# A gated mix of two attention blocks on one core: whole token tiles at the start, fewer closing waits on SyncE, and denominators one group later

## The chip, the cores and the metric

The kernel runs on one core of a Trainium2 chip. A core has five engines that run their own instruction streams side by side: TensorE (PE; its weight loads are listed as PEld), VectorE (DVE), ScalarE (ACT), GpSimd (POOL) and SyncE (SP, which here issues most DMAs). They wait for one another on semaphores. The metric is the device time of one execution in microseconds, lower is better. All tensors are bfloat16; matmuls add up in float32 in PSUM.

## The reference

The input x (1 x 2048 x 1024) goes through two attention blocks of 32 heads of width 32, and the results are mixed by a gate per token:

```python
def _A_ref(x, wqkv, wo):                      # linear attention
    qkv = split_heads(x @ wqkv)
    phi = lambda t: jnp.where(t > 0, t + 1, jnp.exp(t)) + 1e-6
    pq, pk = phi(q), phi(k)
    kv = jnp.einsum("bhsd,bhse->bhde", pk, v)
    z = jnp.einsum("bhsd->bhd", pk)
    num = jnp.einsum("bhqd,bhde->bhqe", pq, kv)
    den = jnp.einsum("bhqd,bhd->bhq", pq, z)[..., None] + 1e-6
    return merge_heads(num / den) @ wo

def _B_ref(x, wqkv, wo):                      # sliding, dilated attention
    W, dil = 8, 2                             # keys at s, s-2, ..., s-14
    ...
    attn = _softmax(logits, axis=-1)
    o = jnp.einsum("bhsw,bhswd->bhsd", attn, vg)
    return merge_heads(o) @ wo

g = _sigmoid((x * gate_w).sum(-1, keepdims=True))
return g * _A_ref(x, A_wqkv, A_wo) + (1 - g) * _B_ref(x, B_wqkv, B_wo)
```

`split_heads` and `merge_heads` stand for the reshapes and transposes.

## The kernel before

**A recorded program with a planner.** `plan` records every operation with `P.op`: its engine, a cost, what it reads and writes, a priority and, for a DMA, a channel (`chan`) with a latency (`lat`). `Prog.schedule` then simulates the five engines with these costs and fixes the order on each one; a DMA is taken to land `lat` after the previous one and a constant 2.0 us more. `Prog.emit` writes the five streams with the semaphore waits that the order needs. Each DMA channel has its own semaphore. The planner runs six times and the shortest plan is kept. So costs and latencies are not code that runs; they only decide the order.

**Stages on PE.** All large products are groups of 8 matmuls of 128 x 512 (L1312), one PSUM bank each.

1. V of block B: 16 token tiles x 2 weight halves (256 matmuls). x comes transposed by DMA into `xT`, as 128-token tiles. Tiles 0 to 3 are loaded as two half tiles of 512 features each (L1299), in the order: first halves of tiles 0, 1, 2, 3, then second halves; tiles 4 to 15 are loaded whole by `load_x` (L1287). The first half of the weights (`load_w`, L1292) comes in four quarters of 256 KB that ACT issues at once; the second half comes in four more that ACT issues behind PE's groups on the first halves of tiles 0 to 3. The order of groups is tiles 0 to 7 on weight half 0, tiles 0 to 7 on half 1, then tiles 8 to 11 and 12 to 15 in the same way. Within tiles 0 to 3, PE does the first half tiles first. Nine matmuls on zeros (L1351) run before. Each group's bank is copied to an SBUF tile by ACT or DVE (L1344, L1343), which SP stores to HBM (L1378).
2. Q and K of block B, then K and V of block A, with the fills of the sliding attention between the groups (L1417, L1436, L1443) and block A's state (L1518).
3. The state is folded into the output weights (L1570). Then come the numerators of block A, 4 chunks of 512 tokens x 8 groups. `after(3, ...)` puts the denominators (L1597) of a chunk three groups behind its last numerator. `over(u)` then takes the reciprocals on ACT, writes them to HBM (L1605, 4 DMAs), reads them back spread over partitions (L1610, 8 DMAs into tiles `rb`), and DVE multiplies the chunk with them (L1613). Groups of `a_out` read the result.
4. The output groups (L1646), DVE's mix (L1650) and the stores of the output (L1656).

**The close.** A flag in SBUF tells whether the data fits the fast path. In `tail` each engine waits for the flag's operation, loads the flag (L1722) and branches (L1726): if the flag is 0, it runs a general path that stands behind the branch in its stream; else it jumps over it, to a drain and a barrier of all engines (L1732). SP, before its branch, waits for the semaphores of all DMA channels (L1725), two in one wait instruction:

```python
if eng == "sp":
    for s, v in P.final:
        e.wait_ge(s, v)
```

The general path starts with waits for all channels and all engines' counts; it does not run with this data.

Of the kernel before, what the change touches and what calls it, by code (L numbers as in the profile page):

```python
# [24 lines left out]
class Tile:  # L25
# [13 lines left out]
    def all(self):  # L39
        return [(self.space, self.lo, self.lo + self.row * self.size, self)]  # L40
# [15 lines left out]


class Op:
    __slots__ = ("eng", "fn", "cost", "deps", "prio", "seq", "chan", "lat", "pos", "val", "users", "raw", "name", "mode", "start", "end")


class Prog:
# [13 lines left out]
        self.held = {}  # L76
        self.read = set()

    def op(self, eng, fn, cost, reads=(), writes=(), prio=None, chan=None, lat=0.0, after=(), name="", mode="m"):
        o = Op()  # L80
        o.eng, o.fn, o.cost, o.prio, o.chan, o.lat, o.name, o.mode = eng, fn, cost, prio, chan, lat, name, mode
        if prio is None:
            o.prio = 1000 + len(self.ops)
        o.seq = len(self.ops)
        o.deps = set(after)
        o.raw = set(after)
        o.users = []
        rd = [iv for r in reads for iv in r]
        wr = [iv for w in writes for iv in w]
        for sp, lo, hi, own in rd:  # L90
            for rec in self.recs.get(sp, ()):
                if rec[0] < hi and lo < rec[1]:
                    if rec[3]:
# [24 lines left out]
        return o  # L118

    def schedule(self, dma_rate=0.2e6):  # L120
# [6 lines left out]
        dma_free = 0.0  # L127
# [20 lines left out]
        while done < len(self.ops):  # L148
            best = None
            for e in self.ENGS:  # L150
                while wait[e] and wait[e][0][0] <= free[e]:
                    _, _, o = heapq.heappop(wait[e])
                    heapq.heappush(avail[e], (o.prio, o.seq, o))
                if avail[e]:
                    t = free[e]
                elif wait[e]:
                    t = wait[e][0][0]
                else:
                    continue
                if best is None or t < best[0]:  # L160
                    best = (t, e)
            assert best is not None, "no operation can go"
            t, e = best
            if not avail[e]:
                while wait[e] and wait[e][0][0] <= t:
                    _, _, o = heapq.heappop(wait[e])
                    heapq.heappush(avail[e], (o.prio, o.seq, o))
            _, _, o = heapq.heappop(avail[e])
            if e == "pe":

                if o.mode != mode and mode != "m":
                    near = [x for x in avail[e] if x[2].mode == mode and x[0] < o.prio + 30]
                    if near:
                        x = min(near)
                        avail[e].remove(x)
                        heapq.heapify(avail[e])
                        heapq.heappush(avail[e], (o.prio, o.seq, o))
                        o = x[2]
                if o.mode != mode:
                    t += 0.09  # L180
                mode = o.mode
            o.start = t
            o.end = t + o.cost
            free[e] = o.end
            fin = o.end
            if o.chan is not None:
                dma_free = max(dma_free, o.end) + o.lat
                fin = dma_free + 2.0
            o.pos = len(self.order[e])
            self.order[e].append(o)  # L190
            done += 1
            for u in o.users:
                lat = self.LAT[o.eng] if (u.eng != o.eng or o in u.raw) and o.chan is None else 0.0
                if u.eng == o.eng == "pe":
                    lat = 0.0
                ready_at[u] = max(ready_at[u], fin + lat)
                left[u] -= 1
                if left[u] == 0:
                    ready(u, ready_at[u])
        self.span = max(free.values())  # L200

    def emit(self, block, tail):
        for e in self.ENGS:
# [40 lines left out]
            tail(e, eng)  # L244

        self.final = [(self.csem[c], n) for c, n in chan_n.items()]
        self.counts = cnt
        block.sync(lambda e: run(e, "sp"))
        block.scalar(lambda e: run(e, "act"))
# [853 lines left out]
def build_kernel(nc, A_x, A_wqkv, A_wo, B_x, B_wqkv, B_wo, gate_w, out):  # L1103
# [117 lines left out]
    def plan(seen):  # L1221
# [68 lines left out]
        def load_w(slot, half, src, c0, prio, d0=0, d1=8, eng="sp", after=()):  # L1290
            n = d1 - d0
            return P.op(eng, lambda e: e.dma_start(ws[slot][:, d0:d1, half * 512:half * 512 + 512], src[:, d0:d1, c0:c0 + 512]), 0.4 + 0.2 * n,  # L1292
                        writes=[ws[slot].part((d0, d1), (half * 512, half * 512 + 512))], prio=prio, chan="w%d_%d_%d" % (slot, half, d0), lat=0.55 * n, after=after)

        for d in range(0, 8, 2):
            load_w(0, 0, Bw, 2048, 0.1 + 0.1 * d, d, d + 2, "act")
        for b in range(2):
            for t in range(4):
                P.op("sp", lambda e, t=t, b=b: e.dma_start_transpose(xT[:, 4 * b:4 * b + 4, t * 128:(t + 1) * 128], x2[0, t * 128:(t + 1) * 128, 512 * b:512 * b + 512]),  # L1299
                     0.8, writes=[xT.part((4 * b, 4 * b + 4), (t * 128, (t + 1) * 128))], prio=4 * b + t, chan="x%d_%d" % (t, b), lat=0.6)  # L1300
        for t in range(4, NT):
            load_x(t, 8 + t)
        P.op("sp", lambda e: e.dma_start(gwb[:, :], gate_w[None, :].to_broadcast([128, D])), 0.6, writes=[gwb.all()], prio=29, chan="gw", lat=0.8)


# [44 lines left out]
        for i in range(WARM):  # L1350
# [2 lines left out]

        early = {(2, 0): (1, 0, Bw, 1024, 21), (4, 1): (2, 0, Bw, 0, 22), (7, 1): (1, 1, Bw, 1536, 23), (10, 1): (2, 1, Bw, 512, 24),
                 (12, 1): (3, 0, Aw, 1024, 25), (14, 1): (3, 1, Aw, 1536, 26)}
        for t, half in [(t, half) for t0, n in ((0, 8), (8, 4), (12, 4)) for half in range(2) for t in range(t0, t0 + n)]:
            vt, vs = vst.next()
            xs, xr = x_tile(t)
            w, wr = w_half(0, half)
            cuts = [0, 8]  # L1360
            if t < 4 and half == 0:
                cuts = [0, 2, 4, 6, 8] if t == 0 else [0, 4, 8]
                if t == 0:
                    first = [main.next() for _ in range(4)]
                    for t_ in range(4):
                        for d, d1 in ((0, 2), (2, 4)) if t_ == 0 else ((0, 4),):
                            group(first[t_], x_tile(t_)[0], w, [xT.part((d, d1), (t_ * 128, t_ * 128 + 128)), ws[0].part((d, d1), (0, 512))], d, d1)
                    o = P.ops[-1]
                    for d in range(0, 8, 2):
                        load_w(0, 1, Bw, 2560, 3 + 0.1 * d, d, d + 2, "act", after=[o])  # L1370
                cuts = cuts[len(cuts) // 2:]
                bank = first[t]
            else:
                bank = main.next()
            for d, d1 in zip(cuts, cuts[1:]):
                o = group(bank, xs, w, [xT.part((d, d1), (t * 128, t * 128 + 128)), ws[0].part((d, d1), (half * 512, half * 512 + 512))], d, d1)
            move(vt[:, :], bank.ap, 512, bank, vt.all())
            P.op("sp", lambda e, t=t, vt=vt, half=half: e.dma_start(vB_hbm[t * 128:(t + 1) * 128, half * 512:half * 512 + 512], vt[:, :]), 0.6, reads=[vt.all()],  # L1378
                 writes=[hb(t * 128, (t + 1) * 128, half)], chan="vst%d" % vs, lat=0.5, prio=5)
# [210 lines left out]
        def over(u):  # L1590
# [16 lines left out]
            for j in range(8):  # L1607
                B, bs = RBr.next()
                src = rc_hbm[u, 4 * j:4 * j + 4, :, :].rearrange("r k n -> (r k) n")[:, None, :].to_broadcast([16, 8, 512])
                last_in[0] = P.op("sp", lambda e, B=B, src=src: e.dma_start(B[:, :], src), 0.5, reads=[[("R", 4 * u + j // 2, 4 * u + j // 2 + 1, None)]], writes=[B.all()],  # L1610
                                  chan="rci%d" % bs, lat=1.0)
                dst, reg = tgt[:, j, c0:c0 + 512], tgt.part((j, j + 1), (c0, c0 + 512))
                P.op("dve", lambda e, B=B, dst=dst: e.tensor_tensor(dst, dst, B[:, :], ALU.mult), 0.65, reads=[reg, B.all()], writes=[reg])  # L1613

# [46 lines left out]
        for n, (u, j) in enumerate(nums):  # L1661
            numer(u, j)
            if j == 7:
                after(3, lambda u=u: over(u))
            slot(0)
            if n in (2, 4, 6, 8):
                fold((n - 2) // 4, (n - 2) // 2 % 2)
# [51 lines left out]
    def tail(e, eng):  # L1719
# [1 line left out]
        e.wait_ge(*flag_op.val)  # L1721
        e.reg_load(reg, flag[0:1, 0:1])  # L1722
        if eng == "sp":
            for s, v in P.final:
                e.wait_ge(s, v)  # L1725
        with e.If_eq(reg, 0):  # L1726
            for s, v in P.final + [(P.esem[x], n) for x, n in P.counts.items() if n]:
# [40 lines left out]
```

## Time and profile before

| | |
|---|---|
| three runs | 499.54, 501.1, 502.52 us (median 501.1) |
| the profiled execution's own time | 499.54 us |
| its span, first to last instruction | 497.7 us |
| PE busy | 484.9 us, 97% of the span |
| DVE, ACT, POOL busy | 274.1, 168.7, 5.1 us |
| granted TensorE clock | 1.000 |
| DMA, mean over the span | 98 GB/s |

The first row is what an execution takes without a profile. The profile lists one execution: its span lies inside the execution's own time, which is 1.84 us longer. Busy time is that of instructions that work; waits, branches and the issuing of DMAs are not counted in it. "Idle before" is the time in which an engine stood still just before an instruction, with what ended it behind an arrow. The first 40th of the span is 12.4 us long; in it PE is busy for 7 tenths, in the last for 5 tenths, and in all between for 9 tenths or more.

### The profile page before, as it was taken

The numbers are of one execution on the slowest core, as the hardware profiler recorded it, in microseconds if no ns is written. First come the engines' busy times: TensorE is split into PE (matmuls) and PEld (weight loads), VectorE is DVE, ScalarE is ACT, GpSimd is POOL, SyncE is SP. The second block draws the span as 40 slices with busy tenths as digits, with TensorE's granted clock in tenths as the row PEclk, the third lists the DMA queues.
The fourth block names the chain that finished last, engine by engine and source line by source line (L and its number), as shares of the span: only waits on it lengthen the run. The fifth ranks groups of instructions, "written<-read, shape, count | busy, mean of one in ns | idle before, by whom it ended". The sixth has DMA issues, their size and how long they took to land.

```text
span 497.7 us, 11467 instructions
## 1 busy us (share of the span) xinstructions
PE 484.9 (97%) x5121; PEld 226.2 (45%) x5121; DVE 274.1 (55%) x484; ACT 168.7 (34%) x290; POOL 5.1 (1%) x27
## 2 busy tenths in 40 slices
PE   7799999999999999999999999999999999999995
PEld 2344444444454444554554454444444444444442
DVE  2211425887777777556554645596865734524443
ACT  1011121133334445565655556355423322020000
POOL 3000000000000000000000000000000000000000
PEclk9999999999999999999999999999999999999999
DMA  8989994133003026301100100501664316101121
GB/s 169 215 192 286 359 353 117 43 107 105 1 24 107 24 79 186 79 24 39 31 24 23 36 12 4 168 3 31 162 190 100 92 24 166 58 8 66 63 86 68
DMA packets 51195, 48.80 MB, mean 98 GB/s; under 512 B 20289, under 2 KB 39105, under 8 KB 51138
## 3 DMA queue, kind: packets, MB, share of 16 engines
q1 hardware_dynamic: 48962, 45.89, 33.0%
q10 hardware_dynamic: 2176, 2.10, 1.9%
q8 instruction: 42, 0.69, 0.6%
q14 instruction: 15, 0.12, 0.1%
HBM read 34.34 MB, written 9.44 MB: 88 GB/s over the span
## 4 chain that ended last, share of the span: by engine, by line
PE 93%; SPq 2%; DMA 2%; DVE 1%; issue 0%
PE ps_all L1312 76%; PE ps_all L1646 11%; PE ps_all L1417 2%; SPq L1299 2%; PE ps_all L1436 2%; DMA xT<-in_A_x_dram 2%; PE ps_all L1518 1%; PE ps_all L1443 1%; DVE zsel L1560 1%; PE ps_all L1597 0%; DVE pq L1325 0%; SPq L1287 0%; PE ps_all L1570 0%; DVE e L1323 0%; DVE w L1343 0%
## 5 line engine op out<-in xcount | busy, mean ns | idle before, releaser
L1312 PE MATMUL ps_all<-w,xT 128*128 128x512 bf16 x960 | 213.9, 379 | 5.9 <-DMA xT<-in_A_x_dram 5.9
L1312 PE MATMUL ps_all<-xT,w 128*128 128x512 bf16 x768 | 170.7, 379 | 0.0
L1312 PEld LDWEIGHTS ps_all<-w,xT 128*128 128x128 bf16 x960 | 91.1, 98 | 115.0 <-DMA xT<-in_A_x_dram 8.5
L1312 PEld LDWEIGHTS ps_all<-xT,w 128*128 128x128 bf16 x768 | 73.7, 98 | 89.1 <-issue 1.8
L1646 PE MATMUL ps_all<-w,qT 128*128 128x512 bf16 (+1 forms) x264 | 55.6, 373 | 0.0
L1646 PEld LDWEIGHTS ps_all<-w,qT 128*128 128x128 bf16 x264 | 25.9, 98 | 29.6
L1323 DVE TENSOR_SCALAR e<-e 128x512 bf16<-128x512 bf16 x64 | 18.3, 290 | 34.6 <-ACT e L1321 17.3
L1343 DVE CAST vst<-ps_all 128x512 bf16<-128x512 f32 x16 | 11.1, 692 | 46.7 <-PE ps_all L1312 46.7
L1423 ACT ACTIVATE E<-ps_all 128x1824 bf16<-128x1824 f32 (+1 forms) x18 | 30.4, 1688 | 9.8 <-PE ps_all L1417 9.0
L1321 ACT ACTIVATE e<-ps_all 128x512 bf16<-128x512 f32 x32 | 19.1, 597 | 42.7 <-PE ps_all L1312 41.6
L1426 DVE TENSOR_TENSOR E<-E,msk 128x1824 bf16<-128x1824 bf16 (+1 forms) x18 | 19.8, 1102 | 22.1 <-ACT E L1423 22.1
L1650 DVE SCALAR_TENSOR_TENSOR o<-ps_all,gm,xT 128x512 bf16<-128x512 f32 (+1 forms) x25 | 18.2, 730 | 23.0 <-PE ps_all L1646 22.8
L1319 ACT ACTIVATE e<-ps_all 128x512 bf16<-128x512 f32 x32 | 19.1, 597 | 26.8 <-PE ps_all L1312 25.8
L1344 ACT ACTIVATE vst<-ps_all 128x512 bf16<-128x512 f32 x16 | 9.5, 597 | 51.1 <-PE ps_all L1312 51.1
L1455 DVE TENSOR_TENSOR qT<-ps_all,L 128x456 bf16<-128x456 f32 (+1 forms) x36 | 21.0, 626 | 6.2 <-ACT L L1453 5.0
L1274 DVE TENSOR_TENSOR mx<-mx,qT 128x1024 bf16<-128x1024 bf16 x32 | 20.9, 687 | 4.2 <-ACT qT L1347 4.0
L1274 DVE TENSOR_TENSOR mx<-mx,kT 128x1024 bf16<-128x1024 bf16 x32 | 20.9, 687 | 3.4 <-ACT kT L1344 3.2
L1344 ACT ACTIVATE kT<-ps_all 128x512 bf16<-128x512 f32 x18 | 10.7, 597 | 34.7 <-PE ps_all L1312 34.7
L1325 DVE SCALAR_TENSOR_TENSOR pk<-ps_all,e 128x512 bf16<-128x512 f32 x32 | 21.9, 687 | 0.7
L1452 ACT ACTIVATE L<-ps_all 128x456 f32<-128x456 f32 (+1 forms) x36 | 17.8, 547 | 12.4 <-PE ps_all L1436 12.4
L1347 ACT ACTIVATE qT<-ps_all 128x512 bf16<-128x512 f32 x18 | 10.8, 597 | 31.1 <-PE ps_all L1312 31.1
L1613 DVE TENSOR_TENSOR xT<-xT,rb 128x512 bf16<-128x512 bf16 x24 | 16.4, 689 | 6.6 <-DMA rb<-rc_hbm 6.3
(72 smaller groups left out, 282.0 us busy)
## 6 DMA issues: line engine op xcount, KB each, us to landing
rb<-rc_hbm SPq DMA_DIRECT2D x32, 256.0 KB, 4.7
w<-in_A_wqkv_dram SPq DMA_DIRECT2D x6, 1024.0 KB, 7.8
v<-vB_hbm SPq DMA_DIRECT2D x36, 128.0 KB, 2.7
vB_hbm<-vst SPq DMA_DIRECT2D x32, 128.0 KB, 6.0
w<-in_B_wqkv_dram SPq DMA_DIRECT2D x4, 1024.0 KB, 7.7
xn<-in_A_x_dram SPq DMA_DIRECT2D x16, 256.0 KB, 2.6
out_dram<-o SPq DMA_DIRECT2D x15, 256.0 KB, 2.0
w<-in_B_wqkv_dram ACTq DMA_DIRECT2D x8, 256.0 KB, 5.1
```

The source lines that it names most:

```text
L1274: P.op("dve", lambda e, m=m, op=op: e.tensor_tensor(m[:, 0:n], m[:, 0:n], src, op), 0.08 + n / 1920.0, reads=[m.all(), reg], writes=[m.all()],
L1312: last = e.matmul(bank.ap(), lhs(dc), rhs(dc), start=(dc == 0), stop=(dc == 7))
L1319: P.op("act", lambda e: e.activation(e_[:, :], bank.ap(), ACT.Exp), act(512), reads=[bank.iv], writes=[e_.all()])
L1321: P.op("act", lambda e: e.activation(e_[:, :], bank.ap(), ACT.Exp, accum_out=qe[:, col:col + 1]), act(512) + 0.1, reads=[bank.iv], writes= ...
L1323: P.op("dve", lambda e: e.tensor_scalar(e_[:, :], e_[:, :], 1.0, 1e-6, op0=ALU.min, op1=ALU.add), 0.25, reads=[e_.all()], writes=[e_.all()])
L1325: P.op("dve", lambda e: e.scalar_tensor_tensor(out=dst, in0=bank.ap(), scalar=0.0, in1=e_[:, :], op0=ALU.max, op1=ALU.add), dps(512), read ...
L1344: fa = lambda e: e.activation(dst, src(), ACT.Copy)
L1423: P.op("act", lambda e: e.activation(E[:, 0:32 * nq].rearrange("p (j q) -> p j q", j=4), ps[:, 4:8, 0:8 * nq], ACT.Exp), act(32 * nq), rea ...
L1426: P.op("dve", lambda e: e.tensor_tensor(ev(), ev(), m[:, :, :].rearrange("p r q -> p (r q)")[:, None, :].to_broadcast([128, 16, 2 * nq]), ...
L1455: P.op("dve", lambda e, L=L, h=h, q0=q0: e.tensor_tensor(qT[:, :, q0:q0 + nq], SO[h].ap(0, n).rearrange("p (c q) -> p c q", c=8), L[:, 0:n ...
L1646: last = e.matmul(bank.ap(0, f1 - f0), qT[:, dc, t * 128:(t + 1) * 128], ws[3][:, dc, f0:f1], start=(dc == 0), stop=(dc == 7))
L1650: P.op("dve", lambda e, bank=bank, o_=o_, t=t, n=n, i0=i0, i1=i1, tgt=tgt, c0=c0: e.scalar_tensor_tensor(out=o_[:, i0 * 128:i1 * 128].rear ...
```

## The change

Three places of the kernel change.

The loads of the start and the order of the V groups. All tiles of x are loaded whole. SP issues tile 0, then the third and fourth quarter of the first weight half, then tiles 1 to 3, then the four quarters of the second weight half, then the other tiles among the stores of V; ACT issues only the first two quarters. The V groups go in blocks of four tiles: four on half 0, the same four on half 1. The first group is cut by quarters, the others are not cut.

```diff
-        for d in range(0, 8, 2):
-            load_w(0, 0, Bw, 2048, 0.1 + 0.1 * d, d, d + 2, "act")
-        for b in range(2):
-            for t in range(4):
-                P.op("sp", lambda e, t=t, b=b: e.dma_start_transpose(xT[:, 4 * b:4 * b + 4, t * 128:(t + 1) * 128], x2[0, t * 128:(t + 1) * 128, 512 * b:512 * b + 512]),
-                     0.8, writes=[xT.part((4 * b, 4 * b + 4), (t * 128, (t + 1) * 128))], prio=4 * b + t, chan="x%d_%d" % (t, b), lat=0.6)
-        for t in range(4, NT):
-            load_x(t, 8 + t)
+        load_x(0, 0)
+        load_w(0, 0, Bw, 2048, 0.1, 0, 2, "act")
+        load_w(0, 0, Bw, 2048, 0.2, 2, 4, "act")
+        load_w(0, 0, Bw, 2048, 0.3, 4, 6)
+        load_w(0, 0, Bw, 2048, 0.4, 6, 8)
+        for t in range(1, NT):
+            load_x(t, 3 + t)
+        for d in range(0, 8, 2):
+            load_w(0, 1, Bw, 2560, 6.1 + 0.1 * d, d, d + 2)
...
-        for t, half in [(t, half) for t0, n in ((0, 8), (8, 4), (12, 4)) for half in range(2) for t in range(t0, t0 + n)]:
+        for t, half in [(4 * b + i, half) for b in range(NT // 4) for half in range(2) for i in range(4)]:
...
-            cuts = [0, 8]
-            if t < 4 and half == 0:
...
-            for d, d1 in zip(cuts, cuts[1:]):
-                o = group(bank, xs, w, [xT.part((d, d1), (t * 128, t * 128 + 128)), ws[0].part((d, d1), (half * 512, half * 512 + 512))], d, d1)
+            step = 2 if t == 0 else 8
+            for d in range(0, 8, step):
+                o = group(bank, xs, w, [xr, ws[0].part((d, d + step), (half * 512, half * 512 + 512))], d, d + step)
```

The denominators of a chunk are recorded four groups behind its last numerator in place of three, and the planner takes the loads of the reciprocals to land 2.5 us later than before:

```diff
-                fin = dma_free + 2.0
+                fin = dma_free + o.pad
...
-                                  chan="rci%d" % bs, lat=1.0)
+                                  chan="rci%d" % bs, lat=1.0, pad=4.5)
...
-                after(3, lambda u=u: over(u))
+                after(4, lambda u=u: over(u))
```

`pad` is 2.0 for every other operation.

SP's closing waits cover only the channels with an operation that nothing waits for. These are four channels, all of stores of the output. Every other channel's DMAs have an operation behind them that waits for them.

```diff
+    def awaited(self, chan):
+
+        return all(o.users for o in self.ops if o.chan == chan)
...
+        self.last = [(self.csem[c], n) for c, n in chan_n.items() if not self.awaited(c)]
...
         if eng == "sp":
-            for s, v in P.final:
+            for s, v in P.last:
                 e.wait_ge(s, v)
```

There were 85 channels before; without the half tiles there are 81.

More of the change, by code (lines that the diff above doesn't have):

```diff
@@ L58 @@
 class Op:
-    __slots__ = ("eng", "fn", "cost", "deps", "prio", "seq", "chan", "lat", "pos", "val", "users", "raw", "name", "mode", "start", "end")
+    __slots__ = ("eng", "fn", "cost", "deps", "prio", "seq", "chan", "lat", "pos", "val", "users", "raw", "name", "mode", "pad", "start", "end")
 class Prog:
@@ L77, in __init__, with op @@
         self.read = set()
-    def op(self, eng, fn, cost, reads=(), writes=(), prio=None, chan=None, lat=0.0, after=(), name="", mode="m"):
+    def op(self, eng, fn, cost, reads=(), writes=(), prio=None, chan=None, lat=0.0, after=(), name="", mode="m", pad=2.0):
         o = Op()
+        o.pad = pad
         o.eng, o.fn, o.cost, o.prio, o.chan, o.lat, o.name, o.mode = eng, fn, cost, prio, chan, lat, name, mode
@@ L1355, in plan @@
                  (12, 1): (3, 0, Aw, 1024, 25), (14, 1): (3, 1, Aw, 1536, 26)}
-        for t, half in [(t, half) for t0, n in ((0, 8), (8, 4), (12, 4)) for half in range(2) for t in range(t0, t0 + n)]:
+        for t, half in [(4 * b + i, half) for b in range(NT // 4) for half in range(2) for i in range(4)]:
             vt, vs = vst.next()
             xs, xr = x_tile(t)
+            bank = main.next()
             w, wr = w_half(0, half)
-            cuts = [0, 8]
-            if t < 4 and half == 0:
[L1362 to L1368, printed above, removed]
-                    for d in range(0, 8, 2):
[L1370 to L1374, printed above, removed]
-            for d, d1 in zip(cuts, cuts[1:]):
-                o = group(bank, xs, w, [xT.part((d, d1), (t * 128, t * 128 + 128)), ws[0].part((d, d1), (half * 512, half * 512 + 512))], d, d1)
+            step = 2 if t == 0 else 8
+            for d in range(0, 8, step):
+                o = group(bank, xs, w, [xr, ws[0].part((d, d + step), (half * 512, half * 512 + 512))], d, d + step)
             move(vt[:, :], bank.ap, 512, bank, vt.all())
```

## The prediction

> **What bounds the kernel now.** I read first the page's busy shares (PE 97%), then the groups of instructions for idle time in front of PE's matmuls. Idle time is the number after the second bar:
>
> ```profile
> L1312 PE MATMUL ps_all<-w,xT 128*128 128x512 bf16 x960 | 213.9, 379 | 5.9 <-DMA xT<-in_A_x_dram 5.9
> ```
>
> All idle time that the matmul groups show is these 5.9 us, waits for x. The gaps lie in the first 20.3 us; from there to the last matmul PE stops once, for 0.055 us. So an edit can win only at the start, or after the last matmul. The timeline of PE at the start (start, us, count, idle before it):
>
> ```profile
> 4.64 0.63 PE L1351 MATMUL ps_all<-warm 128*128 128x512 bf16 x1
> 6.04 1.04 PE L1312 MATMUL ps_all<-w,xT 128*128 128x512 bf16 x4 [0.77 <-DMA xT<-in_A_x_dram]
> 8.79 6.22 PE L1312 MATMUL ps_all<-w,xT 128*128 128x512 bf16 x28 [1.70 <-DMA xT<-in_A_x_dram]
> 16.27 1.90 PE L1312 MATMUL ps_all<-w,xT 128*128 128x512 bf16 x8 [1.27 <-DMA xT<-in_A_x_dram]
> 20.30 2.98 PE L1312 MATMUL ps_all<-w,xT 128*128 128x512 bf16 x13 [2.13 <-DMA xT<-in_A_x_dram]
> ```
>
> The last row gives the pitch: (2.98 - 0.38)/12 = 0.216 us a matmul. At 20.30 us 40 are done, worth 8.64 us, so PE works as if it had started at 11.66 us and never stopped. I call that the effective start. Why x is late stands in SP's timeline and in three stretches (PE, PEld, DVE, ACT, POOL busy; granted clock; DMA share; GB/s):
>
> ```profile
> 0.80 10.51 SPq L1299 DMA_TRANSPOSE xT<-in_A_x_dram  x8
> 11.35 9.17 SPq L1287 DMA_TRANSPOSE xT<-in_A_x_dram  x4
> ```
>
> ```profile
> 2.00:8.00 6.00, 4.31 (x12) 1.22 (x10) 1.68 (x7) 1.28 (x1) 3.20 (x15) 1.00 1.13 234
> 9.00:14.00 5.00, 5.00 (x25) 2.27 (x24) 1.38 (x2) 0.00 (x0) 0.00 (x0) 1.00 0.59 128
> 14.00:20.00 6.00, 2.90 (x13) 0.97 (x11) 1.39 (x3) 0.60 (x1) 0.00 (x0) 1.00 1.17 240
> ```
>
> A half tile costs SP 10.51/8 = 1.3 us to issue, and so does a whole one (1.31 us unhindered). Eight halves hold SP until 11.3 us while DMA moves only 128 GB/s between 9 and 14 us, against 234 to 240 when both queues are full. Tile 4 is issued only then, and tiles 4 and 5 share the DMA with the second weight half, which ACT issues at 11.59: hence the gaps before 16.27 and 20.30.
>
> At the end, the last DVE row ends at 492.57 us, the span at 497.67. Between them stand these instructions (name, count, ns min/median/max, first and last start):
>
> ```profile
> L1725 SPq EVENT_SEMAPHORE  x42: 27/28/28, 493.9 to 496.8; - x42
> ```
>
> ```profile
> L1726 POOLq COMPARE_BRANCH  x1: 45/45/45, 436.5 to 436.5; - x1
> L1726 ACTq COMPARE_BRANCH  x1: 50/50/50, 447.7 to 447.7; - x1
> L1726 PEldq COMPARE_BRANCH  x1: 3524/3524/3524, 490.3 to 490.3; - x1
> L1726 DVEq COMPARE_BRANCH  x1: 72/72/72, 492.7 to 492.7; - x1
> L1726 SPq COMPARE_BRANCH  x1: 58/58/58, 496.9 to 496.9; - x1
> ```
>
> ```profile
> L1732 POOLq DRAIN  x1: 108/108/108, 439.0 to 439.0; - x1
> L1732 ACTq DRAIN  x1: 80/80/80, 450.3 to 450.3; - x1
> L1732 PEldq DRAIN  x1: 73/73/73, 493.9 to 493.9; - x1
> L1732 DVEq DRAIN  x1: 59/59/59, 495.6 to 495.6; - x1
> L1732 SPq DRAIN  x1: 57/57/57, 497.4 to 497.4; - x1
> ```
>
> 42 waits of two semaphores each take SP from 493.90 to 496.86 (0.07 us apiece). The last output lands at 495.08. SP's drain is the last of the five.
>
> **The change, part by part.** *Loads at the start.* Four issues of whole tiles replace eight of halves: 4 x 1.3 = 5.2 us less on SP. Six of the eight quarter weight loads come to SP from ACT, each about 0.54 us by ACT's median issue: 3.2 us more, but the last four no longer wait for PE's first groups. SP is through with tiles 0 to 3 and the weights at 0.8 + 1.3 + 2 x 0.54 + 3 x 1.3 + 4 x 0.54, with 0.05 us between, or 9.7 us. That is faster than DMA can move it: 12 pieces of 256 KB are 3.15 MB, at the 234 GB/s of 2 to 8 us 13.4 us. DMA starts at 2 us (7 GB/s before), so the last quarter of the second weight half comes at 15.4, and lands, I say, by 16.0. PE's own chain: tile 0 with the first weight half needs about the 8.4 us at which that half landed before, plus 128 KB more of x; tile 1 I put at 9.6. From there the new order (four tiles on one half, then on the other) gives PE 24 matmuls for tiles 1 to 3 and 6 for tile 0's second half: 9.6 + 30 x 0.216 = 16.1. So the 39th matmul starts at 16.1, and the effective start is 16.1 - 38 x 0.216 = 7.9: **3.7 us earlier**. Bounds: at 200 GB/s, the slowest 2 us with both queues full (6 to 8 us), the last quarter lands near 18.3, effective start 10.1, gain 1.6; with tile 1 at 9.0 and nothing else late, 7.3, gain 4.4. I take 3.7 because the long stretches (234, 240) agree.
>
> What is late next: tile 4 stands on SP behind the first store of V, which waits for ACT's copy of the first group (done near 10). Store 0.58, so tile 4's issue starts near 10.6. Whole tiles landed 3.5 to 7.8 us behind the start of their issue (median 4.6): 18.4 at worst. PE wants tile 4 at 7.9 + 64 x 0.216 = 21.7. The cover is 3.3 us at worst and 6.5 at the median; beyond it each us costs one. Weights for the next stage are wanted 55 us after the effective start, at 63; issued around 35 and landing in 7.8, they are at nothing, and what hides them is some 20 us of V groups.
>
> *Denominators one group later; longer latency assumed.* Counting PE's instructions in both programs, their order differs behind the folds alone: the first denominator comes 8 matmuls later, the second at the same place, the third 3 groups later, the fourth at the same place; work is equal. Before, the last reciprocal of chunk 0 landed at 357.14, its DVE product ended at 357.85, and the first group that reads it ran at 361.06. Now the product ends 1.73 later and the group 1.73 later: 3.2 us of cover, as before. The other chunks have over 10 us. PE has no gap there to win, and DVE's 6.3 us of waits for reciprocals lie beside it. Cost 0; bounds 0 and, if the landing grew from its median 4.7 by more than the cover, some us. Nothing seen goes past the 5.8 maximum, so 0.
>
> *Closing waits.* Two wait instructions remain, on the last outputs. SP then sits at 495.08 + 0.1 instead of 496.86, and branches to 495.2. What follows has two prices in the rows. SP's branch ended at 496.95, its drain began at 497.40: 0.45. DVE needed 495.56 - 492.75 = 2.81, ACT 2.57, POOL 2.49, each with one 8192-byte instruction packet 0.9 us behind its branch. SP had its packet at 495.62, before it branched, a moment after a pause of 0.37 us among the waits, in front of SP's 206th instruction. In the new program the branch is the 201st: it comes before that place, and jumps over 145 instructions. So I expect no packet under way, and 2.49 to 2.81: drain at 497.7 to 498.0, end 0.28 later (57 ns of drain, 0.22 from there to the span's end, as before), against 497.67: a **loss of 0.3 to 0.6, taken as 0.45**. With 0.45 us it would be a gain: drain end 495.7, just behind DVE's 495.62, end 495.9, 1.75 less.
>
> [...]
>
> **Sum.** -3.7 + 0 + 0.45 = -3.2 us. The profiled execution took 499.54 us, 1.84 of it around the span, so 496.3 by it. It was the fastest of three; from the median 501.1 it is **497.9**. Bounds of the terms: -4.4 + 0.3 = -4.1 to -1.6 + 0.6 = -1.0, so 497.0 to 500.1 for this case.
>
> **The rivals.** *SP finds its code at hand* (0.22): -3.7 - 1.75 = -5.4, 495.7. For: SP took 0.45 before. Against: four engines did not, and the packet's place.
>
> *SP's queue backs up* (0.12, slower). With two whole tiles outstanding, the third and fourth of the x4 row needed 2.61 and 3.82 us instead of 1.31. If tiles 1 to 3 each take 3.82, SP is through at 9.7 + 7.5 = 17.2, and the last quarter lands, with ACT's slowest 7.0 us behind the end of its issue, at 24.2: effective start 16.0, 4.3 lost, 0.45 more in the tail, 505.9. It decides from a landing at 19.9 (no gain) or 21.9 (slower by more than 2.5 us). Against: DMA stays full while SP is held, so bytes, not issues, set the landing.
>
> *A stall behind the folds* (0.11): a reciprocal late by 2 us over the cover gives back 2 of the 3.2: 499.9. For: DVE waits there already. Against: 3.2 us of cover.
>
> *Forecast* 0.55.
>
> **How the numbers follow.** Faster means over 0.5% (2.5 us), about what a measurement of this kernel can tell from none; its three runs span 3 us. The forecast's own range reaches past -2.5 in most of it: 0.40 faster, 0.15 same. With the first rival 0.22 faster; the stall 0.11 same; the backed-up queue 0.11 slower, 0.01 same: 0.62, 0.27, 0.11. The range takes in the first rival less the runs' scatter (494.5) and the forecast's slow bound with it (501.5); it leaves most of the backed-up queue out.
>
> **What would show it.** Right: no second gap of over 1 us behind 10 us, the 40th matmul near 16.5, last matmul near 488.3, five drains with SP's 2.5 us behind its branch. Wrong: PE waiting for the second weight half beyond 18.3; a gap before the first L1312 group on the reciprocals; SP's drain within 0.5 us of its branch.

## The result

Six executions of the changed kernel have a median of 495.53 us (495.31 to 496.11); six of the kernel before 501.99 us (499.54 to 503.08). The ratio is 0.9879 with a 95% interval of 0.9855 to 0.9902: faster by 6.46 us. The profiled execution took 495.88 us, 1.74 of it beyond its span of 494.14. From profile to profile the time fell by only 3.66 us, since the profiled execution of the kernel before (499.54) was the fastest of its six.

First the group of V's matmuls in the changed kernel (busy us, mean ns; idle before them and what ended it), then PE's timeline at the start (start, us, count, idle):

```profile
L1319 PE MATMUL ps_all<-w,xT 128*128 128x512 bf16 x960 | 215.1, 381 | 0.7 <-DMA xT<-in_A_x_dram 0.7
```

```profile
1.25 4.02 PE L1358 MATMUL ps_all<-warm 128*128 128x512 bf16 x9 [1.25 <-DVE warm L1272]
5.97 24.30 PE L1319 MATMUL ps_all<-w,xT 128*128 128x512 bf16 x104 [0.70 <-DMA xT<-in_A_x_dram]
```

5.9 us of idle time have become 0.7. Behind 5.97 us PE doesn't wait for a load again; its one later stop is 0.06 us long, as before. The last matmul ends at 488.05 in place of 492.05, and all of these 4.0 us are there by the 41st V matmul (16.30 in place of 20.30). Three stretches of the start (PE, PEld, DVE, ACT, POOL busy; granted clock; DMA share; GB/s) and SP's queue in the same time:

```profile
2.00:8.00 6.00, 5.30 (x13) 1.65 (x12) 1.68 (x7) 1.05 (x1) 3.21 (x15) 1.00 1.08 283
9.00:14.00 5.00, 5.00 (x24) 2.25 (x23) 0.69 (x1) 1.20 (x2) 0.00 (x0) 1.00 1.05 285
14.00:20.00 6.00, 6.00 (x30) 2.69 (x29) 0.69 (x1) 1.25 (x3) 0.00 (x0) 1.00 0.95 208
```

```profile
3.35 4.97 SPq L1293 DMA_TRANSPOSE xT<-in_A_x_dram  x3
8.36 2.12 SPq L1298 DMA_DIRECT2D w<-in_B_wqkv_dram  x4
11.03 3.64 SPq L1293 DMA_TRANSPOSE xT<-in_A_x_dram  x2
```

Between 9 and 14 us, where eight half tiles had let DMA fall to 128 GB/s, it now moves 285. SP is through with everything up to the second weight half at 10.5. Tile 1 landed at 8.14, tile 3 at 10.27, the four quarters of the second weight half at 11.80 to 14.36, tile 4 at 15.84.

PE nevertheless starts slowly. The clock column has its first record at 9.43 us in this execution and shows 1.00 before it, so the count of matmuls has to tell:

```profile
5.97:9.42 3.45, 3.45 (x9) 1.25 (x10) 0.00 (x0) 0.00 (x0) 0.00 (x0) 1.00 1.14 275
9.42:12.87 3.45, 3.45 (x18) 1.56 (x17) 0.00 (x0) 1.20 (x2) 0.00 (x0) 1.00 0.92 269
```

PE is busy throughout both, with 9 matmuls in the first and 18 in the second: 0.427 us apart up to 9.43, half the clock, and 0.216 from there on.

At the end, the waits, branches and drains (ns min/median/max, first and last start):

```profile
L1719 SPq EVENT_SEMAPHORE  x2: 17/22/28, 491.1 to 491.3; - x2
```

```profile
L1720 DVEq COMPARE_BRANCH  x1: 72/72/72, 488.7 to 488.7; - x1
L1720 SPq COMPARE_BRANCH  x1: 58/58/58, 491.3 to 491.3; - x1
```

```profile
L1726 DVEq DRAIN  x1: 58/58/58, 491.6 to 491.6; - x1
L1726 SPq DRAIN  x1: 63/63/63, 493.9 to 493.9; - x1
```

Two waits in place of 42. SP branches at 491.34, 0.09 us behind the landing of the last output (491.25), and its drain comes 2.46 us behind the end of the branch, where it had been 0.45; its packet of instructions comes at 492.28, behind the branch. From the last matmul to the span's end it is 6.09 us, against 5.62 before.

### The profile page after: what moved, and what is told of

It reads as the page before. It is cut to its first block, busy times and chain, and to the rows that moved or that the text cites. A ratio compares the mean times of both kernels' runs of the same rounds, so it can differ in the third digit from the quotient of the medians.

```text
span 494.1 us, 11425 instructions
## 1 busy us (share of the span) xinstructions
PE 486.0 (98%) x5121; PEld 226.8 (46%) x5121; DVE 273.7 (55%) x486; ACT 167.7 (34%) x288; POOL 5.1 (1%) x27
## 4 chain that ended last, share of the span: by engine, by line
PE 96%; DVE 2%; DMA 1%; issue 0%
PE ps_all L1319 78%; PE ps_all L1640 11%; PE ps_all L1411 2%; PE ps_all L1430 2%; DMA xT<-in_A_x_dram 1%; PE ps_all L1512 1%; PE ps_all L1437 1%; DVE zsel L1554 1%; PE ps_all L1591 0%; DVE pq L1332 0%; PE ps_all L1564 0%; DVE e L1330 0%; DVE w L1350 0%; DVE o L1644 0%; DVE kvT L1550 0%
## 5 line engine op out<-in xcount | busy, mean ns | idle before, releaser
L1446 ACT ACTIVATE L<-ps_all 128x456 f32<-128x456 f32 (+1 forms) x36 | 17.8, 547 | 12.4 <-PE ps_all L1430 12.4
L1351 ACT ACTIVATE kT<-ps_all 128x512 bf16<-128x512 f32 x16 | 9.6, 597 | 35.8 <-PE ps_all L1319 35.8
L1354 ACT ACTIVATE xT<-ps_all,g 128x512 bf16<-128x512 f32 x14 | 9.3, 686 | 35.6 <-PE ps_all L1319 35.6
L1354 ACT ACTIVATE qT<-ps_all 128x512 bf16<-128x512 f32 x16 | 9.6, 597 | 31.5 <-PE ps_all L1319 31.5
```

Source lines behind the costliest of these rows:

```text
L1351: fa = lambda e: e.activation(dst, src(), ACT.Copy)
L1354: fa = lambda e: e.activation(dst, src(), ACT.Copy, scale=scale)
```

## The experiments

### The kernel before again

No edit; the same program in another profiled execution.

> The kernel before, once more. Its six executions took 499.5 to 503.1 us, those of the changed kernel only 495.3 to 496.1; the profiled execution was its fastest. Theory A: that scatter belongs to its start, where PE works in bursts between waits, and the slow half clock lasts longer in most executions than in the profiled one (there to 5.9 us): then a second profile shows an effective start some 1 to 3 us later than 11.66 us with a longer stretch of clock 0.5, and the same time (5.6 us) from the last matmul to the end. Theory B: the scatter belongs to DMA landings: the clock rises as early, and the gaps before matmuls on x are longer. Theory C: it is the chip and not the kernel: this run's executions lie within 1 us of each other.

Measured: 502.68 us median (501.06 to 504.41, 12 executions) against 501.48 (500.38 to 504.72, 29) of the kernel before beside it, ratio 1.0005 [0.9984, 1.0026]. This profiled execution took 504.0 us, and its start looks unlike the first one's (PE's timeline, then two stretches of it):

```profile
7.90 9.63 PE L1312 MATMUL ps_all<-w,xT 128*128 128x512 bf16 x36 [1.37 <-DMA xT<-in_A_x_dram]
20.27 1.90 PE L1312 MATMUL ps_all<-w,xT 128*128 128x512 bf16 x8 [2.75 <-DMA xT<-in_A_x_dram]
24.27 1.94 PE L1312 MATMUL ps_all<-w,xT 128*128 128x512 bf16 x6 [2.10 <-DMA xT<-in_A_x_dram]
```

```profile
8.10:11.40 3.30, 3.30 (x9) 1.21 (x8) 0.00 (x0) 0.00 (x0) 0.00 (x0) 0.50 0.42 90
25.20:28.50 3.30, 3.30 (x9) 1.13 (x8) 0.69 (x1) 0.00 (x0) 0.00 (x0) 0.50 0.96 270
```

In both stretches PE is busy all the time and gets half its matmuls done: the granted clock is 0.50 from 8.06 to 11.47 and from 25.13 to 28.54. Each costs half of 3.41 us. The last matmul ends at 496.46, 4.41 later than in the first profile: some 3.4 by the clock, 0.8 by longer waits, and 0.39 at a place that had no gap before, ahead of the third chunk's denominators, less 0.25 for an earlier rise of the clock:

```profile
379.38 0.62 PE L1597 MATMUL ps_all<-xT,zsel 128*32 128x512 bf16 x8 [0.39 <-DVE xT L1325]
```

So the same program has a better and a worse start, and the profile that I predicted from was a good one. Theory A had the half clock right and its place wrong: the first rise came earlier (4.65), and the lost intervals lie behind later stops. The stops are longer too, as in theory B, and the scatter stayed (theory C falls).

### The start alone

The loads and the order of the V groups as changed; SP's closing waits on all channels, `after(3)` and the old latency kept.

> The start of the change alone: whole tiles, weights on SP, groups in blocks of four; closing waits on all 81 channels, denominators as before. The prediction's terms: all of the gain at the start, so it should be as fast as the changed kernel or 0.5 us faster, since SP's branch stands behind the place where its packet is fetched (237th instruction): last matmul to end 5.6 us, SP's branch to its drain 0.45 us. Rival (the closing waits bring part of the gain): 1 to 2 us slower than the changed kernel.

Measured: 495.46 us (494.80 to 496.95, 6 executions), ratio 0.9863 [0.9833, 0.9892]: as much as the whole change. The last matmul ended at 487.98, SP's drain came 0.45 us behind its branch, and from the last matmul to the span's end it was 5.65 us. In front of the third chunk's denominators PE stood still for 0.53 us. PE's start:

```profile
8.03 6.22 PE L1319 MATMUL ps_all<-w,xT 128*128 128x512 bf16 x28 [0.20 <-DMA xT<-in_A_x_dram]
14.42 11.93 PE L1319 MATMUL ps_all<-w,xT 128*128 128x512 bf16 x53 [0.18 <-DMA w<-in_B_wqkv_dram]
```

### The closing waits alone

```diff
-            for s, v in P.final:
+            for s, v in P.last:
```

> The closing waits of the change alone, 4 channels of 85, on the start of before. The branch becomes SP's 197th instruction, ahead of the 206th. Prediction's theory: SP's drain 2.4 to 2.8 us behind its branch, last matmul to end 6.1 us against 5.6: 0.5 us slower than before, which is inside the noise of before's times, so the profile decides. Rival (SP finds its code at hand): drain 0.45 us behind the branch, last matmul to end 3.8 us, 1.8 us faster.

Measured: 502.1 us (500.70 to 505.02, 12), ratio 1.0005 [0.9982, 1.0027]. The tail grew to 6.18 us, with SP's drain 2.51 us behind its branch (499.95 to 502.46):

```profile
L1731 SPq COMPARE_BRANCH  x1: 58/58/58, 499.9 to 499.9; - x1
L1737 SPq DRAIN  x1: 57/57/57, 502.5 to 502.5; - x1
```

Over all profiles of this study, the six with all closing waits have tails of 5.62 to 5.88 us (mean 5.75), the six with four channels and no instructions added to SP 6.03 to 6.71 (mean 6.30). The 0.5 us of the tail are plain in the traces and too small for the medians.

### The denominators alone

`after(4)` and `pad=4.5` put into the kernel before.

> Denominators one group later and the longer latency for the reciprocals' loads alone. Prediction's theory: no change of time; PE shows no gap over 0.1 us between 25 us and its last matmul; DVE's waits on the reciprocals fall below the 6.9 us of before or stay. Rival: a gap on PE before the first group on the reciprocals, 0.5 to 3 us.

Measured: 500.87 us (499.82 to 504.02, 12), ratio 0.9991 [0.9969, 1.0013]: no difference. Its profile has no gap ahead of the denominators. Over all profiles the third chunk's denominators had a gap of 0.39, 0.53, 0.70 and 0.71 us in four of the six profiles with `after(3)`, and none in any of the eight with `after(4)`. The edit removes a stop of about half a microsecond that some executions have.

### SP's next code asked for early

The changed kernel with 24 more semaphore waits on SP, which make 12 more instructions, on channels that have long landed, ahead of the last ten operations, so that the branch stands later in SP's stream. Nothing is left out.

```diff
             for k, (o, waits) in enumerate(plan[eng]):
+                if eng == "sp" and k == len(plan[eng]) - 10:
+                    for s, v in met:
+                        e.wait_ge(s, v)
```

> The changed kernel with 24 waits more on SP, for loads that landed long before, in front of its tenth last DMA. There SP has time to spare. The branch becomes the 213th instruction, behind the 206th, where the packet with the code behind the branch is asked for. Theory (the branch waits for its code): drain 0.45 us behind SP's branch instead of 2.46, last matmul to end 4.0 to 4.1 us instead of 6.1, so about 2 us faster than the changed kernel: 493.5. Rival (the wait has to do with the two waits that remain, or with any jump of SP): still 2.4 to 2.5 us, no gain.

Measured: 494.4 us (494.19 to 494.70, 6), ratio 0.9845 [0.9809, 0.9882]. Branches and drains of DVE and SP:

```profile
L1725 DVEq COMPARE_BRANCH  x1: 72/72/72, 487.9 to 487.9; - x1
L1725 SPq COMPARE_BRANCH  x1: 58/58/58, 490.6 to 490.6; - x1
```

```profile
L1731 DVEq DRAIN  x1: 58/58/58, 490.8 to 490.8; - x1
L1731 SPq DRAIN  x1: 57/57/57, 491.1 to 491.1; - x1
```

SP's packet came at 482.89, during the outputs, and its drain 0.45 us behind its branch: only the place of the branch was changed, and 2.0 us left the span (4.08 us from the last matmul to its end, against 6.09). Not all of it counts. The execution's own time now lies 3.00 us beyond the span, not 1.74. DVE, whose drain ends at 490.87, has its next packet of instructions only at 491.40, and the closing events, which stop at 491.87, go on at 493.17. The changed kernel's closing events have no such pause (0.23 us at most): there DVE's drain ended at 491.62 and SP's began at 493.86, so that a pause of that length would lie beside SP's. 1.26 of the 2.0 us come back; 0.7 to 1.1 stay, and the 493.5 us expected were missed. That some stays is clear: the slowest execution here (494.70) lies under the fastest of the run with 13 matmuls on zeros beside it (494.85).

### Thirteen matmuls on zeros

```diff
-    WARM = 9
+    WARM = 13
```

> The changed kernel with 13 matmuls on zeros ahead instead of 9. In its profile the clock stood at 0.5 until 9.43 us and 8 matmuls of the first tile took 0.427 us apart. Theory (a gap on PE decides when the clock rises): PE is busy from 1.25 to 6.4 without a gap, the clock is at 1.0 by 8.1 at the latest, and the last matmul comes 0 to 1 us earlier. Rival: the first group only waits for the added matmuls, 0.5 to 0.9 us later.

Measured: 495.17 us (494.85 to 495.25, 6), ratio 0.9859 [0.9822, 0.9895]. The clock rose at 5.88, PE went from zeros to V without a pause, and the last matmul ended at 486.72, 1.33 earlier than in the changed kernel's profile:

```profile
1.25 5.25 PE L1358 MATMUL ps_all<-warm 128*128 128x512 bf16 x13 [1.25 <-DVE warm L1272]
6.33 20.03 PE L1319 MATMUL ps_all<-w,xT 128*128 128x512 bf16 x92
```

That is the theory's way, somewhat beyond its 0 to 1 us. The time fell by 0.36 at most: this execution's tail is 6.71 us, with 2.81 from SP's branch to its drain. Both edits together:

> Both additions. If they do not touch each other: the sum of what they bring, 493 to 493.5 us, and the fastest so far.

Measured: 494.46 us (494.32 to 494.68, 6), ratio 0.9848 [0.9812, 0.9884], last matmul at 487.16: no better than the early code alone, and not the 493 to 493.5 expected. The two are the fastest kernels of this study, 0.7 to 1.1 us below the two medians of the changed kernel (495.1 and 495.53). The extra zeros gain nothing that can be measured, since the changed kernel gets its early rise of the clock in other executions anyway (at 6.27 us in its second profile, below).

### Zeros in the gaps of the kernel before

The kernel before with 6, 8 and 8 matmuls on zeros where PE waits for x, so that it is never idle for long. They are extra work; the computation is whole.

> The kernel before with 22 matmuls on zeros put into the gaps of its start: 6 behind tile 0's first half, 8 ahead of tile 4's group, 8 ahead of tile 5's (0.216 us each, 4.75 us in all, in gaps of 1.4 to 3.2 us). Theory (most executions of before lose time since the gaps let the clock fall to half for one or more stretches of 3.41 us): the clock stays at 1.0 after its first rise, the executions lie near 499.5 and within 1.5 us of each other, 2 us faster than before's median. Rival (the scatter is the DMA landings): the same 500.4 to 504.7 us as before, or slower by the matmuls added.

Measured: 500.73 us (500.20 to 502.42, 12) against 501.26 (499.58 to 505.45, 17), ratio 0.9979 [0.9954, 1.0005]. From 5.93 on the clock stayed at 1.0:

```profile
14.63 1.89 PE L1318 MATMUL ps_all<-warm 128*128 128x512 bf16 x8
16.84 1.90 PE L1312 MATMUL ps_all<-w,xT 128*128 128x512 bf16 x8 [0.32 <-DMA xT<-in_A_x_dram]
18.58 1.89 PE L1318 MATMUL ps_all<-warm 128*128 128x512 bf16 x8
20.99 5.35 PE L1312 MATMUL ps_all<-w,xT 128*128 128x512 bf16 x24 [0.52 <-DMA xT<-in_A_x_dram]
```

The clock did what the theory said, and all twelve executions have a mean clock of 0.997 or more; the time did not. The spread shrank from 5.9 to 2.2 us, while the median fell by 0.5 in place of 2, and the interval takes in no change at all: the 41st V matmul starts 0.69 later than in the first profile of before (20.30), and this execution had the 0.70 us gap ahead of the denominators. Over 110 executions with the old start (the kernel before, again, the closing waits alone, the denominators alone) the mean clock of an execution runs from 0.986 to 0.999, and the time falls with it, by 0.31 us per 0.001 (correlation -0.73); at 0.999 the mean is 500.8, over all 502.0. The mean clock also counts the fall behind the last matmul, which costs nothing: in the changed kernel's profile the clock falls at 490.71, 2.67 us behind the last matmul, and that alone makes 0.997. One interval of 3.41 us at half clock takes 0.0034 off the mean, so executions at 0.997 or more had, by this estimate, none at the start: 25 of the 110, with a mean of 501.0 us. Filling the gaps (mean 500.9) makes every execution like these, and no faster.

### Whole tiles alone

The kernel before with tiles 0 to 3 loaded by four issues in place of eight:

```diff
-        for b in range(2):
-            for t in range(4):
-                P.op("sp", lambda e, t=t, b=b: e.dma_start_transpose(...), ...)
-        for t in range(4, NT):
+        for t in range(NT):
             load_x(t, 8 + t)
```

> The kernel before with one edit: tiles 0 to 3 are loaded whole (four issues by SP in place of eight); the weights stay on ACT and the order of the groups as before. Theory (SP's issuing of eight half tiles is what makes x late): SP is through with tiles 0 to 3 by about 6 us in place of 11.3, tile 4 is issued there and lands by 13, tile 5 by 15, and what PE still waits for is the second weight half alone, which ACT issues behind PE's groups: gaps behind 10 us of at most 1 us in place of 3.4, last matmul at 488.5 to 490, 496 to 498 us. Rival (the place and order of the weights and the order of the groups matter as much): a gap of over 1.5 us stays behind 10 us, last matmul at 490 to 492, 498 to 500.5 us.

Measured: 502.69 us (499.63 to 506.03, 12) against 501.73 (500.14 to 506.52, 19), ratio 1.0024 [0.9994, 1.0054], last matmul at 492.86. Both expectations fall: the gap behind 10 us is 1.34, and the time did not move. PE's timeline, ACT's issue of the second weight half, and the stretch from 9 to 14 us:

```profile
6.09 1.04 PE L1308 MATMUL ps_all<-w,xT 128*128 128x512 bf16 x4 [0.81 <-DMA xT<-in_A_x_dram]
9.64 14.53 PE L1308 MATMUL ps_all<-w,xT 128*128 128x512 bf16 x59 [2.51 <-DMA xT<-in_A_x_dram]
25.50 6.86 PE L1308 MATMUL ps_all<-w,xT 128*128 128x512 bf16 x30 [1.34 <-DMA w<-in_B_wqkv_dram]
```

```profile
16.43 2.09 ACTq L1292 DMA_DIRECT2D w<-in_B_wqkv_dram  x4
```

```profile
9.00:14.00 5.00, 4.36 (x14) 1.70 (x15) 0.16 (x1) 0.60 (x1) 0.00 (x0) 0.66 1.09 203
```

DMA is kept full now, but with the wrong pieces. Tile 1 lands at 9.59 (8.14 in the changed kernel), behind all four quarters of the first weight half and beside tile 2. Tiles 4 to 8 go ahead of the second weight half, which ACT issues at 16.43, behind PE's work, and whose last quarter lands at 25.46. The stop of 2.51 us is followed by half the clock until 12.51. Total stops are 1.2 us shorter than in the first profile of before; the half clock (1.7 us) and a gap ahead of the denominators (0.71) take more than that. SP was not through with tiles 0 to 3 by 6 us either, but at 9.2: the issues of tiles 2 and 3 took 2.93 and 2.40 us.

### The changed kernel with half tiles

The changed kernel with tiles 0 to 3 as eight half loads in the same places.

> The changed kernel with tiles 0 to 3 loaded as eight half tiles again, everything else as changed. Theory (issuing is what counts): SP needs some 5 us more, issues the second weight half from 11.5 to 15 us, its last quarter lands at 17 to 18.5 in place of 14.4, and PE stops for 1.5 to 3 us ahead of tile 0's second half: last matmul at 489.5 to 491.5, 497 to 499 us. Rival (DMA's bytes set the landing, the number of issues doesn't matter): no gap behind 7 us, 495 to 496 us.

Measured: 499.08 us (498.29 to 500.08, 8), ratio 0.9949 [0.9932, 0.9966], last matmul at 490.87. The theory holds, a little above its range: 4.0 us slower than the changed kernel beside it.

```profile
13.96 2.33 PE L1327 MATMUL ps_all<-w,xT 128*128 128x512 bf16 x10 [0.89 <-DMA xT<-in_A_x_dram]
16.59 0.61 PE L1327 MATMUL ps_all<-w,xT 128*128 128x512 bf16 x2 [0.30 <-DMA w<-in_B_wqkv_dram]
17.58 0.60 PE L1327 MATMUL ps_all<-w,xT 128*128 128x512 bf16 x2 [0.39 <-DMA w<-in_B_wqkv_dram]
18.68 13.55 PE L1327 MATMUL ps_all<-w,xT 128*128 128x512 bf16 x60 [0.50 <-DMA w<-in_B_wqkv_dram]
```

```profile
9.00:14.00 5.00, 3.84 (x17) 1.45 (x18) 0.69 (x1) 0.70 (x2) 0.00 (x0) 1.00 0.42 94
```

SP issues half tiles until 12.4 us, and between 9 and 14 us DMA moves only 94 GB/s. The second weight half is issued from 12.42 on, and its last quarter lands at 18.64. PE takes it quarter by quarter: in the changed kernel both groups of tile 0 are cut by quarters, and not the first alone.

### The changed kernel again

> The changed kernel, on the chip of the two others, to compare them with: 495.3 to 496.1 us in every run. Theory of the clock (the granted clock steps on a grid of 3.41 us whose place differs between executions, and rises or not behind the nine matmuls on zeros by how that grid lies): the rise is at 5 to 6.5 us or near 9.4, with the last matmul at 486.5 or 488.0. Rival (the profiled execution was out of the ordinary): neither of the two.

Measured, beside the two above: 495.1 us (494.59 to 496.64, 5), ratio 0.9874 [0.985, 0.9899]. The clock rose at 6.27, the last matmul ended at 486.83:

```profile
5.71 2.15 PE L1319 MATMUL ps_all<-w,xT 128*128 128x512 bf16 x8 [0.44 <-DMA xT<-in_A_x_dram]
8.04 24.17 PE L1319 MATMUL ps_all<-w,xT 128*128 128x512 bf16 x109 [0.18 <-DMA xT<-in_A_x_dram]
```

This is the early rise that the theory of the clock allowed. The time's range was missed at both ends, by 0.7 and 0.5 us.

### The old order of groups

The changed kernel with the order of the V groups recorded as before (tiles 0 to 7 on half 0, then on half 1).

> The changed kernel with the old order of the V groups (tiles 0 to 7 on weight half 0, then on half 1, then 8 to 11 and 12 to 15); loads on the same engines in the same places as changed. What PE wants behind its first 32 V matmuls, near 14.6 us, is then tile 4 in place of the second weight half. Theory (which engine issues the second weight half, and ahead of which tiles, is what counts; the order of groups only decides which piece is late): tile 4 lands near 15.8 and tiles 5 to 7 up to 21.5, PE stops for 1 to 2.5 us in all behind 10 us, last matmul at 488 to 489.5 (486.8 to 488.0 with the new order), 496 to 497.5 us. Rival (the new order carries most of the gain, since it needs only four tiles until both halves are there): stops of over 3 us behind 10 us, last matmul at 490 or later, 498.5 us or more.

Measured: 495.1 us (494.80 to 495.56, 5), ratio 0.9849 [0.9827, 0.9872], last matmul at 486.99. Both missed: there is no stop behind 8.2 us.

```profile
8.16 27.12 PE L1319 MATMUL ps_all<-w,xT 128*128 128x512 bf16 x122 [0.19 <-DMA xT<-in_A_x_dram]
```

I had argued from the recorded order. The planner puts two groups of half 1 behind tile 3 and then tiles 4 to 7. Tile 4 landed at 16.24, and PE came to it at 16.8. The changed kernel's trace has the same order: PE comes to tile 4 behind 48 matmuls, not 64. The planner makes the order of the start from the loads, whatever the loop says; the edit of the loop is worth nothing here.

## Why the prediction was right, and where it was not

*The loads at the start: right, by two errors that cancel.* The recorded 3.7 us against 4.0 in the profile, effective start 7.66 for 7.9. "... tile 1 I put at 9.6" was too late: tile 1 landed at 8.14. PE nevertheless came to it only at 9.34, because the eight matmuls of tile 0 took 0.427 us apiece, 1.69 us more than the working had for them; from there 30 x 0.216 us did hold. That the two errors met is luck. "At the 234 GB/s of 2 to 8 us 13.4 us" was too slow as well: DMA moved 283 GB/s from 2 to 8 us and 285 from 9 to 14, and the second weight half was there at 14.4, not 16.0. Without the slow matmuls the start is worth 4.7 to 5.3 us: so much earlier than before the 41st V matmul starts in the six other profiles with this start and whole tiles, where the clock rose early.

*Which piece of it does the work: less simple than "eight halves hold SP".* Whole tiles in the old arrangement gained nothing (1.0024 [0.9994, 1.0054]), the new arrangement with half tiles 0.5% (0.9949 [0.9932, 0.9966], with the other two edits in it), both together 1.3% (0.9874 [0.985, 0.9899]). Four issues in place of eight free SP, and that pays only when what SP issues next is what PE wants next. That the second weight half no longer waits for PE was in the working, as a minor clause.

*What is late next: nothing, as forecast, but by less than the working had.* Tile 4 was issued at 11.03 and landed at 15.84. "PE wants tile 4 at 7.9 + 64 x 0.216 = 21.7" took the order from the loop; PE came to it behind 48 matmuls, at 17.8. The cover was 2.0 us in place of 3.3 to 6.5, and only 0.5 to 0.6 in those six profiles (start alone, early code, extra zeros, both, again, old order). A start faster by more than that would find PE waiting for tile 4, unless the tile comes earlier too. A longer issue with tiles outstanding did appear (tile 2's took 2.2 us, against the 2.6 to 3.8 that I had read), and nothing waited for it: the rival of the queue that backs up fell.

*The closing waits: right in mechanism and size.* Recorded +0.45, measured +0.47 in the changed kernel and about +0.5 alone. That the branch's place against the next packet of code decides it is shown by the run with 12 instructions more: same branch, as SP's 213th instruction, 0.45 us. With half tiles it is the 205th, still ahead of the 206th, and the drain came 2.54 us behind it. The rival that SP finds its code at hand fell for this kernel, and its price was too high in any case: it counted 1.75 us of gain in the span, of which 1.26 would have come back behind it. Over the runs the drain came 2.46 to 2.81 us behind a branch that stood ahead of the 206th instruction, and 0.45 us behind a later one (kernel before, start alone, early code).

*The denominators: 0 was right by the medians, its reason not quite.* "PE has no gap there to win" held for the profile that I had; other executions of the same order stop there for 0.39 to 0.71 us. The stall behind the folds did not come.

*The sum: right from profile to profile, mis-sized from median to median.* Recorded -3.2; the spans differ by 3.53 and the medians by 6.46. The step that failed is "from the median 501.1 it is 497.9": it carries a difference between two single executions over to the median. The profiled execution of before had granted clock 1.000 and lay 2.45 us under its median; the changed kernel's lay 0.35 above its own. The measured 495.53 lies beside the 495.7 of the rival in which SP finds its code at hand, by chance: SP waited 2.46 us.

The change also took away stops after which the clock fell, by the mean clock, in most executions of before (under 0.997 in 85 of the 110). By the 110 executions, those without such a fall lie 1.1 us under the mean of all (501.0 against 502.0). That is an estimate of their share in the 2.45 us; it is read off executions that differ in other ways too, and no run isolates it. The rest, longer waits and the denominators' gap, was seen in two profiles and not counted over many executions; how it divides stays open.

## What to carry to other kernels

Read more than one profiled execution where the time scatters, and look at the granted clock behind each stop: a stop of 2 to 3 us can cost 1.7 us more afterwards (the one of 2.51 us with whole tiles alone: 3.41 us at half the clock), and a change that removes stops removes that too. Fewer issues help only as far as the freed queue carries the piece that is wanted next, so list landings beside the times at which they are wanted. A wait that seems useless at the end of a stream can be what lets the next packet of code arrive (the drain 0.45 us behind SP's branch with 42 closing waits, 2.51 with the closing waits alone changed), and a gain inside the span counts only after what lies behind the span has been looked at (with the early code 1.26 of 2.0 us came back there).

## What had not been expected of the hardware

The granted clock changed only on a grid of 3.413 us: in the kernel before it stood at 1.0 for 491.52 us (5.92 to 497.44), in the changed kernel for 481.28 (9.43 to 490.71), 144 and 141 times that. The grid's place differed between executions: the clock first rose at 4.65 to 6.71 us in 13 of the 14 profiles, at 9.43 in the changed kernel's first. With each 128x512 matmul counted at its 0.216 us, an interval of the grid at full clock in which PE stood idle for 2.2 us or more of 3.41 was followed by half the clock: five intervals at the start, with 2.2 to 2.5 us (two of the kernel before again, two of the closing waits alone, one of whole tiles alone). Those with 2.0 us or less were not (2.0 in the kernel before, 5.92 to 9.33). The profile's own idle time, which begins at a matmul's modelled end, does not part the two: 1.83 us was followed by half the clock in one profile (the kernel before again, 4.65 to 8.06) and not in another (the kernel before, 5.92 to 9.33). The half clock lasted one interval, where PE was then busy; with 1.1 us idle in it, it lasted a second (the closing waits alone, 22.58 to 29.40). An interval idle for some two thirds of its length was enough.

A transposing DMA of a half tile took SP as long to issue (1.3 us) as one of a whole tile, and some issues of whole tiles with others outstanding took 1.7 to 3.9 us at the start (2.22 for tile 2 of the changed kernel and 2.61 and 3.81 in the kernel before, with two outstanding; 2.07 for tile 5 of the changed kernel, with one). Others in the same place did not: tile 3 of the changed kernel was issued in 1.31 us with tiles 1 and 2 outstanding. What decides it stays open.

Two pauses stood at the end. Where SP's packet came behind its branch (492.28 behind 491.34 in the changed kernel), the drain came 2.46 to 2.81 us behind the branch. And in the run with the early code the closing events, outside the span, went on only about 2.3 us behind DVE's drain (490.87 to 493.17), whose packet came at 491.40.
